# A retention layer and a PReLU feed-forward layer: the second product of blocks 1 to 5 computed as seven products of quarters

## The chip, the cores and the metric

The kernel runs on one core of a Trainium2 chip. The metric is the device time of one launch in microseconds (us), lower is better. Engines are named as the profile names them: PE (TensorE, matmuls), PEld (its weight loads), DVE (VectorE), ACT (ScalarE), POOL (GpSimd), SP (SyncE, which here only issues DMAs).

## The reference

Inputs are float32: q, k and v of 4 batches, 8 heads, 768 steps and 64 channels; two weight matrices of 512 x 2048 and 2048 x 512; and a vector alpha of 2048. The output is float32, 3072 x 512.

```python
# first layer, for each batch b and head h
state = gamma[h] * state + outer(k[t], v[t])
y[t] = scale * q[t] @ state
# second layer, over the 3072 tokens x (heads side by side)
h = x @ w_in
g = max(h, 0) + alpha * min(h, 0)
out = g @ w_out
```

## The kernel before

**Tiling.** The sequence of each batch is cut in three units of 256 steps, 12 units in all. Two units make a block of 512 tokens, so there are six blocks, n = 0 to 5. Matrix inputs are in 16 bits (float16), sums in PSUM in 32 bits. PSUM has eight banks of 128 x 512 32-bit values; the kernel names the bank of every tile by hand.

**First layer, per unit u.** `load(u)` reads k, q and v by DMA (SP). `rescale` multiplies k and q by powers of gamma into `kdq`, and `cast_v` makes `vx` in 16 bits (mostly POOL). `turn_pe` (early units) or `turn_dma` (a transposing DMA on SP's queue, from unit 4 on) makes the transposed `kq`. `sum_mm` makes the unit's two state sums (tiles `st0`, `st1`); `state` adds them on DVE to the running state (`ss`), multiplies by the decay on POOL (`tf`) and casts the result into `tg` (POOL or ACT). `score_mm` makes the scores of half the heads in two banks, and `masks` multiplies these on DVE by the causal mask. `out_mm` multiplies state and masked scores out, and `take_y` copies the result to `xT` on ACT.

**Second layer, per block n.** `ffn1(n)` makes 16 chunks of h (tile `hps`, four matmuls each). For each, ACT writes `hm` = relu(-h), and DVE writes a chunk of `gt` = hm x (1 - alpha) + h, which is g. Chunks of the first blocks are in part made one unit at a time, with 256 columns (`apart`). `ffn2(n)` multiplies: for each of four groups of 128 tokens (tq), 16 matmuls of 512 columns over the chunks of `gt`, a copy to `os` on ACT, and a store on SP's queue. In block 5 the last group is made in two halves of 256 columns.

**Order.** The kernel writes the order of every engine by hand (`manual_schedule`): each engine carries out its instructions in the order in which the program issues them. The tile library adds semaphore waits where data or buffers need them; a tile with `bufs=k` has k buffers in turn, and the tile after k others waits until all use of the first is over. `ffn1` and `ffn2` are generators that yield after each matmul; `tick(gen, m)` runs m of them, and so places the first layer's work for the next block between the matmuls of the second layer. The stretch at the end of block 0 matters here: there `ffn2(0)` (generator `gen`), the parts of `ffn1(1)` (generator `half`) and the first layer of units 2 and 3 alternate, and on SP's queue `turn_dma(4)` and `load(6)` stand ahead of the four stores of block 0.

**Tiles.** `os` has six buffers, the staged `ks`, `qs` and `vs` four each, `gt` two, `hm` three.

Of the kernel before, what the change touches and what calls it, by code (L numbers as in the profile page):

```python
# [20 lines left out]
def kernel(  # L21
# [68 lines left out]

    tgbuf = [sbp.tile([128, NP, 128], F16, tag=f"tg{i}", name=f"tg{i}") for i in range(6)]

    staged, prepped, live, tgs, xT, gts = {}, {}, {}, {}, {}, {}
    held = []

    def hold(ins):
        if held:
# [9 lines left out]
    def load(u, parts="kqv"):  # L107
        b, c = divmod(u, UPB)
        t = staged.setdefault(u, {})
        for nm in parts:  # L110
            src = {"k": k, "q": q, "v": v}[nm[0]]
            if nm[0] not in t:
                t[nm[0]] = sbp.tile(
                    [128, H, 2 * D], FP, tag=f"{nm[0]}s", bufs=4, name=f"{nm[0]}s{u}"
                )
            h = slice(0, H) if len(nm) == 1 else slice(4 * int(nm[1]), 4 * int(nm[1]) + 4)
            hold(
                nc.sync.dma_start(  # L118
                    out=t[nm[0]][:, h, :],
                    in_=src[b, h, U * c : U * c + U, :].rearrange(  # L120
                        "h (p r) d -> p h (r d)", r=2
                    ),
                )
            )
# [10 lines left out]
    def rescale(eng, u, t, h0, h1):  # L135
        kdq = unit(u)[0]
        at = OQ * t
        eng.tensor_tensor(  # L138
            out=kdq[:, t, :, h0:h1, :].rearrange("p r h d -> p h r d"),
            in0=staged[u]["kq"[t]][:, h0:h1, :].rearrange("p h (r d) -> p h r d", r=2),  # L140
            in1=tab[:, at + 2 * h0 : at + 2 * h1]
            .rearrange("p (h r) -> p h r", r=2)
            .unsqueeze(3)
            .to_broadcast([128, h1 - h0, 2, D]),
            op=MULT,
        )
# [160 lines left out]
    def take_y(u, cs):  # L307
# [4 lines left out]
        for c in cs:  # L312
# [7 lines left out]
                scale=1.0,  # L320
            )

    def ffn1(n, banks, apart=0):
# [5 lines left out]
        turns += [(f, 1, 0, 2) for f in range(apart, NFT)]  # L329
        for i, (f0, nf, lo, hi) in enumerate(turns):  # L330
            hps = ps(banks[i % len(banks)], "hps").rearrange("p (f t) -> p f t", f=nf)
            for f in range(nf):
                for hp in range(4):
                    nc.tensor.matmul(  # L334
                        out=hps[:, f, :].rearrange("p (u t) -> p u t", t=U),
                        lhsT=w_in_all[:, hp, 128 * (f0 + f) : 128 * (f0 + f) + 128],
                        rhs=xT[n][:, lo:hi, hp, :],
                        start=(hp == 0),
                        stop=(hp == 3),
                    )  # L340
# [4 lines left out]
            nc.scalar.activation(out=hm, in_=hps, func=RELU, bias=0.0, scale=-1.0)  # L345
            for f in range(nf):
                nc.vector.scalar_tensor_tensor(  # L347
                    out=gt[:, f0 + f, U * lo : U * hi],
                    in0=hm[:, f, :],
                    scalar=oma_sb[:, f0 + f : f0 + f + 1],  # L350
                    in1=hps[:, f, :],
                    op0=MULT,
                    op1=ADD,
                )
            yield

    def ffn2(n, banks, parts=1):
        gt = gts.pop(n)
        opss = {}
        step = NFT // parts  # L360
        for f0 in range(0, NFT, step):
            for tq in range(3 if n == NBLK - 1 else 4):
                if f0 == 0:
                    opss[tq] = ps(banks[tq % len(banks)], "ops")
                for ft in range(f0, f0 + step):
                    nc.tensor.matmul(  # L366
                        out=opss[tq],
                        lhsT=gt[:, ft, 128 * tq : 128 * tq + 128],
                        rhs=w_out_all[:, ft, :],
                        start=(ft == 0),  # L370
                        stop=(ft == NFT - 1),
                    )
                    if ft == NFT - 1:
                        os_sb = sbp.tile([128, d_model], FP, tag="os", bufs=6, name="os")
                        nc.scalar.activation(  # L375
                            out=os_sb, in_=opss[tq], func=COPY, bias=0.0, scale=1.0
                        )
                        row = TB * n + 128 * tq
                        nc.sync.dma_start(out=out[row : row + 128, :], in_=os_sb)
                    yield  # L380

        if n < NBLK - 1:
            return

        row = TB * n + 384
        for half in range(2):
            ops = ps(banks[1 + half], "ops")[:, 0:256]
            for ft in range(NFT):
                nc.tensor.matmul(  # L389
                    out=ops,  # L390
                    lhsT=gt[:, ft, 384:512],
                    rhs=w_out_all[:, ft, 256 * half : 256 * half + 256],
                    start=(ft == 0),
                    stop=(ft == NFT - 1),
                )
                yield
            for x in range(half + 1):
                w = 256 // (half + 1)
                os_sb = sbp.tile([128, d_model], FP, tag="os", bufs=6, name="os")[:, 0:w]
                i = ops[:, w * x : w * x + w]  # L400
                if x == 0:
                    nc.scalar.activation(out=os_sb, in_=i, func=COPY, bias=0.0, scale=1.0)
                else:
                    nc.vector.tensor_copy(out=os_sb, in_=i)
                at = 256 * half + w * x
                (nc.sync, nc.scalar)[x].dma_start(
                    out=out[row : row + 128, at : at + w], in_=os_sb
                )
# [137 lines left out]
    masks(3, 0)  # L546
    sum_mm(3, (6, 7))
    state(3, 0, G, "ga")
    tick(gen, 8)
    score_mm(3, 1, (4, 5))  # L550
    masks(3, 1)
    rescale(G, 4, 0, 0, 8)
    state(3, 1, G)
    rescale(G, 4, 1, 0, 8)
    cast_v(G, 4)
    turn_dma(4)
    load(6)
    rescale(G, 5, 0, 0, 8)
    rescale(G, 5, 1, 0, 8)
    cast_v(G, 5)  # L560
    tick(gen, 8)
    out_mm(3, (6, 7))
    tick(gen)
    turn_dma(5)
    load(7)
    tick(half)


    for n in range(1, NBLK):
# [36 lines left out]


# [28 lines left out]
```

## Time and profile before

| | |
|---|---|
| median of three runs | 212.03 us (211.62 to 212.3) |
| the profiled execution | 212.65 us, of it 210.9 us span from first to last instruction |
| TensorE's granted clock | 1.000 on average |
| busy | PE 202.7 us (96%), DVE 118.0 (56%), ACT 98.8 (47%), POOL 82.6 (39%) |
| second product (L366, L389) | 368 matmuls of 512 columns, 32 of 256 |
| first product (L334) | 336 matmuls of 512 columns, 96 of 256 |

The profile is one execution. Busy time of PE counts a matmul from its start to its modelled end, and matmuls overlap: the time from start to start, or the length of a run of them in the chain, says what each costs. Instruction groups give the source line, engine, operation, shapes, count, busy time and mean nanoseconds of one, and then the idle time of the engine ahead of them. In a timeline the first two numbers are start and length in us.

### The profile page before, as it was taken

The page shows a single profiled execution, that of the slowest core. Times are in us where ns is not written, and L with a number is a line of the kernel's source. Part 1 is how long each engine was busy: PE and PEld are TensorE (multiplying, and loading weights), DVE is VectorE, ACT ScalarE, POOL GpSimd, SP SyncE. Part 2 cuts the span into 40 slices and gives each one's busy share as a digit, 9 for nine tenths or more (in the row PEclk, how much of TensorE's full clock was granted, in tenths as well). Part 3 has the DMA queues.
Part 4 walks back from the last instruction along what each step waited for, and adds up shares of the span by engine and source line. Part 5 has one row for each costly group of instructions (what it writes and reads, how often), then busy time and mean ns, then how long its engine had stood idle before and what let it go on. Part 6 is the DMA issues. An engine that isn't in the chain of part 4 may idle for free.

```text
span 210.9 us, 4992 instructions
## 1 busy us (share of the span) xinstructions
PE 202.7 (96%) x2090; PEld 106.7 (51%) x2090; DVE 118.0 (56%) x194; ACT 98.8 (47%) x160; POOL 82.6 (39%) x104
## 2 busy tenths in 40 slices
PE   7799999997999999999999999999999999999993
PEld 2457545583564555444555444555444555444462
DVE  7785986354378831488740488740588640588000
ACT  2375665362667132666133566133665133665121
POOL 2389066464791599100499300499100610000000
PEclk9999999999999999999999999999999999999999
DMA  5999999999969991599521599521630111100112
GB/s 164 338 215 150 211 271 163 226 264 314 284 164 368 209 356 64 138 289 262 163 104 50 149 289 242 183 88 53 171 79 0 50 57 50 50 0 3 50 70 79
DMA packets 62407, 33.91 MB, mean 161 GB/s; under 512 B 18081, under 2 KB 59441, under 8 KB 62385
## 3 DMA queue, kind: packets, MB, share of 16 engines
q1 hardware_dynamic: 57840, 29.30, 48.8%
q0 software_dynamic: 4224, 4.19, 12.5%
q8 instruction: 16, 0.26, 0.5%
q10 hardware_dynamic: 320, 0.10, 0.2%
q14 instruction: 7, 0.05, 0.1%
HBM read 27.30 MB, written 6.29 MB: 159 GB/s over the span
## 4 chain that ended last, share of the span: by engine, by line
PE 77%; DMA 16%; POOL 1%; ACT 1%; DVE 1%; SPq 1%; issue 1%; POOLq 0%
PE ops L366 34%; PE hps L334 31%; DMA vs<-in_v_dram 5%; DMA wout<-in_moe_w_out_dram 4%; DMA ks<-in_k_dram 4%; DMA win<-in_moe_w_in_dram 3%; PE y L295 2%; PE kps L87 2%; PE ops L389 2%; PE y L280 2%; PE sca L251 2%; PE st L201 1%; ACT kq L174 1%; SPq L118 1%; PE scb L251 1%
## 5 line engine op out<-in xcount | busy, mean ns | idle before, releaser
L347 DVE SCALAR_TENSOR_TENSOR gt<-hm,oma,hps 128x512 f16<-128x512 f32 (+1 forms) x108 | 73.1, 688 | 50.9 <-ACT hm L345 41.9
L334 PE MATMUL hps<-xT,win 128*128 128x512 f16 (+1 forms) x432 | 84.3, 355 | 0.0
L366 PE MATMUL ops<-wout,gt 128*128 128x512 f16 x368 | 83.7, 379 | 0.0
L345 ACT ACTIVATE hm<-hps 128x512 f32<-128x512 f32 x96 | 57.3, 597 | 26.4 <-PE hps L334 26.3
L334 PEld LDWEIGHTS <-win 128*128 128x128 f16 x432 | 42.1, 98 | 40.8
L366 PEld LDWEIGHTS <-gt 128*128 128x128 f16 x368 | 34.5, 98 | 40.2
L375 ACT ACTIVATE os<-ops 128x512 f32<-128x512 f32 x23 | 13.6, 599 | 52.9 <-PE ops L366 52.9
L226 POOL TENSOR_TENSOR tf<-ss,tab 128x256 f32<-128x256 f32 x16 | 10.2, 636 | 44.6 <-DVE ss L225 44.0
L263 DVE TENSOR_TENSOR m<-sca,mi 128x512 f16<-128x512 f32 x24 | 16.5, 686 | 17.3 <-PE scb L251 17.3
L138 POOL TENSOR_TENSOR kdq<-ks,tab 128x1024 f16<-128x1024 f32 (+1 forms) x12 | 19.3, 1612 | 7.8 <-DMA ks<-in_k_dram 7.5
L239 POOL CAST tg<-tf 64x256 f16<-64x256 f32 x35 | 13.8, 394 | 21.2 <-DVE tf L222 19.5
L313 ACT ACTIVATE xT<-y 128x512 f16<-128x512 f32 x24 | 16.2, 740 | 11.1 <-PE y L295 11.1
L138 POOL TENSOR_TENSOR kdq<-qs,tab 128x1024 f16<-128x1024 f32 (+1 forms) x13 | 20.4, 1571 | 1.7 <-DMA qs<-in_q_dram 1.5
L154 POOL CAST vx<-vs 128x1024 f16<-128x1024 f32 (+1 forms) x13 | 12.6, 972 | 9.7 <-DMA vs<-in_v_dram 9.7
L263 DVE TENSOR_TENSOR m<-scb,mi 128x512 f16<-128x512 f32 x24 | 16.3, 681 | 0.0
L174 ACT ACTIVATE kq<-trb 128x1024 f16<-128x1024 f16 x8 | 8.2, 1022 | 5.9 <-PE trb L168 5.8
L87 PE MATMUL kps<-spin 128*128 128x512 f16 x25 | 8.5, 480 | 1.9 <-DVE spin L432 1.5
L225 DVE TENSOR_TENSOR ss<-tf,st 128x256 f32<-128x256 f32 x16 | 6.7, 416 | 5.7 <-PE st L201 4.8
L251 PE MATMUL sca<-kq 64*64 64x128 f16 x192 | 8.2, 218 | 1.2 <-ACT kq L174 1.1
L251 PE MATMUL scb<-kq 64*64 64x128 f16 x192 | 8.3, 219 | 0.0
L251 PEld LDWEIGHTS <-kq 64*64 64x64 f16 x384 | 6.1, 106 | 4.2 <-ACT kq L174 2.9
L295 PE MATMUL y<-m,vx 64*64 64x128 f16 x384 | 7.7, 219 | 0.0
(33 smaller groups left out, 67.7 us busy)
## 6 DMA issues: line engine op xcount, KB each, us to landing
out_dram<-os SPq DMA_DIRECT2D x23, 256.0 KB, 2.0
vs<-in_v_dram SPq DMA_DIRECT2D x10, 512.0 KB, 6.5
ks<-in_k_dram SPq DMA_DIRECT2D x8, 512.0 KB, 4.5
qs<-in_q_dram SPq DMA_DIRECT2D x8, 512.0 KB, 5.4
ks<-in_k_dram SPq DMA_DIRECT2D x8, 256.0 KB, 5.1
qs<-in_q_dram SPq DMA_DIRECT2D x8, 256.0 KB, 5.2
win<-in_moe_w_in_dram POOLq DMA_DIRECT2D x4, 512.0 KB, 5.8
wout<-in_moe_w_out_dram POOLq DMA_DIRECT2D x4, 512.0 KB, 9.1
```

Source lines behind the costliest of these rows:

```text
L87: nc.tensor.matmul(out=pt, lhsT=spin[:, 0:128], rhs=spin, start=True, stop=True)
L138: eng.tensor_tensor(out=kdq[:, t, :, h0:h1, :].rearrange("p r h d -> p h r d"), in0=staged[u]["kq"[t]][:, h0:h1, :].rearrange("p h (r d) - ...
L154: eng.tensor_copy(out=o, in_=i)
L239: nc.gpsimd.tensor_copy(out=o, in_=i)
L251: nc.tensor.matmul(out=scs[a][rows(c), at : at + 128], lhsT=kv[rows(a), 0, r, p, rows(c)], rhs=qmove(kq, a, c, p), start=True, stop=True,)
L263: nc.vector.tensor_tensor(out=m2, in0=live[u, hh][a].rearrange("p (r a i) -> p r a i", r=2, a=2), in1=mask.unsqueeze(2).to_broadcast([128, ...
L313: nc.scalar.activation(out=xT[n][:, ul, :, 128 * c : 128 * c + 128].rearrange("k a (p r) -> k a r p", r=2), in_=ys[c].rearrange("k (a r p) ...
L334: nc.tensor.matmul(out=hps[:, f, :].rearrange("p (u t) -> p u t", t=U), lhsT=w_in_all[:, hp, 128 * (f0 + f) : 128 * (f0 + f) + 128], rhs=x ...
L345: nc.scalar.activation(out=hm, in_=hps, func=RELU, bias=0.0, scale=-1.0)
L347: nc.vector.scalar_tensor_tensor(out=gt[:, f0 + f, U * lo : U * hi], in0=hm[:, f, :], scalar=oma_sb[:, f0 + f : f0 + f + 1], in1=hps[:, f, :],
L366: nc.tensor.matmul(out=opss[tq], lhsT=gt[:, ft, 128 * tq : 128 * tq + 128], rhs=w_out_all[:, ft, :], start=(ft == 0), stop=(ft == NFT - 1),)
L375: nc.scalar.activation(out=os_sb, in_=opss[tq], func=COPY, bias=0.0, scale=1.0)
```

## The change

From block 1 on `ffn2_seven` takes the place of `ffn2`. It cuts g in four quarters by units and by halves of d_ff, and w_out in four by halves of d_ff and d_model, and makes the block's output from seven products of quarters (Strassen's scheme in Winograd's form), each of 16 matmuls of 256 columns. Where the scheme adds products, TensorE adds into the same bank (0 or 1), ACT keeps a copy of what is there (`cu`), and DVE adds two of them (`plus`) into `os`. Four sums of quarters of w_out are made once on DVE (`w_sums`, tile `wsum`), four sums of quarters of g in each block (`g_sums`, which share the two buffers of `gt`).

With this, `ffn1` makes its chunks in the order 0, 8, 1, 9 and so on for n > 1 and has another list of banks; the tick counts, the banks of `out_mm` and `score_mm`, and the place of `state`, `masks` and `rescale` in the program change; a `rescale` in each block is made to wait for the last sum on DVE (`behind`); two `cast_v` move to ACT; `os` goes from six buffers to three, and the staged tiles from four to three. Block 5's output ends in `last`.

```diff
-                    [128, H, 2 * D], FP, tag=f"{nm[0]}s", bufs=4, name=f"{nm[0]}s{u}"
+                    [128, H, 2 * D], FP, tag=f"{nm[0]}s", bufs=3, name=f"{nm[0]}s{u}"
...
+    def w_sums(i, lo, hi):
+        w = w_out_all.rearrange("p (k f) (j e) -> p k f j e", k=2, j=2)
+        w12, w21, w22 = w[:, 0, lo:hi, 1, :], w[:, 1, lo:hi, 0, :], w[:, 1, lo:hi, 1, :]
+        t1, t2, t3, t4 = (wsum[:, x, lo:hi, :] for x in range(4))
+        o, a, b = (
+            (t1, w12, w[:, 0, lo:hi, 0, :]), (t2, w22, t1), (t3, w22, w12), (t4, w21, t2)
+        )[i]
+        return nc.vector.tensor_tensor(out=o, in0=a, in1=b, op=SUB)
...
+    def g_sums(n, i, lo, hi):
+        if n not in gsums:
+            gsums[n] = sbp.tile([128, 4, HF, U], F16, tag="gt", bufs=2, name=f"gs{n}")
...
+        o, a, b, op = (
+            (s1, a21, a22, ADD), (s2, s1, a11, SUB), (s3, a11, a21, SUB), (s4, a12, s2, SUB)
+        )[i]
+        return nc.vector.tensor_tensor(out=o, in0=a, in1=b, op=op)
...
+        rest = range(apart, NFT)
+        if apart == 0:
+            rest = [f + x for f in range(HF) for x in (0, HF)]
...
+            if n > 0 and f0 in (HF + 5, NFT - 1):
+                lo, hi = (0, 6) if f0 < NFT - 1 else (6, HF)
+                g_sums(n, 0, lo, hi)
+                g_sums(n, 1, lo, hi)
             yield
...
-                        os_sb = sbp.tile([128, d_model], FP, tag="os", bufs=6, name="os")
+                        os_sb = sbp.tile([128, d_model], FP, tag="os", bufs=3, name="os")
...
+    def ffn2_seven(n, x, y, z=None):
...
+        ox = bank(x, "ox")
+        yield from product(ox, gq(0, 0), wq(0, 0), True)
+        c1 = kept(ox)
+        yield
+        oy = bank(y, "oy")
+        yield from product(oy, gq(1, 0), wq(1, 0), True)
+        store(0, 0, plus(oy, c1))
+        yield
+        yield from product(ox, gs(1), ws(1), False)
+        u2 = kept(ox)
+        yield
+        oy = bank(y, "oy")
+        yield from product(oy, gs(0), ws(0), True)
+        if z is not None:
+            u5 = plus(oy, u2, "cu")
+        yield
+        yield from product(ox, gs(2), ws(2), False)
+        u3 = kept(ox)
+        store(1, 1, plus(oy, u3))
+        yield
+        if z is not None:
+            oz = bank(z, "oz")
+            yield from product(oz, gs(3), wq(1, 1), True)
+            store(0, 1, plus(oz, u5))
+            yield
+            yield from product(ox, gq(1, 1), ws(3), False, lambda m: last(n, ox, m))
+            yield
+        else:
+            yield from product(ox, gq(1, 1), ws(3), False)
...
+            store(1, 0, c21)
+            yield
+            yield from product(oy, gs(3), wq(1, 1), False)
+            store(0, 1, plus(oy, u2))
+            yield
...
     state(3, 0, G, "ga")
+    w_sums(0, 0, HF)
+    for i in range(1, 4):
+        w_sums(i, 0, 4)
     tick(gen, 8)
     score_mm(3, 1, (4, 5))
     masks(3, 1)
-    rescale(G, 4, 0, 0, 8)
     state(3, 1, G)
+    for i in range(1, 4):
+        gate = w_sums(i, 4, HF)
+    behind(rescale(G, 4, 0, 0, 8), gate)
     rescale(G, 4, 1, 0, 8)
-    cast_v(G, 4)
+    cast_v(A, 4)
     turn_dma(4)
     load(6)
...
-    cast_v(G, 5)
     tick(gen, 8)
     out_mm(3, (6, 7))
     tick(gen)
     turn_dma(5)
     load(7)
+    tick(half, 8)
+    cast_v(A, 5)
     tick(half)
...
-            gen = ffn1(n, (4, 5, 6, 7, 0, 1))
+            gen = ffn1(n, (7, 2, 3, 1, 0, 6, 5, 4, 7, 1, 0, 4, 5, 6, 7, 1))
             if more:
                 for u in (u0, u0 + 1):
-                    tick(gen, 8)
-                    rescale(G, u, 0, 0, 8)
+                    i = rescale(G, u, 0, 0, 8)
+                    if u == u0:
+                        behind(i, gate)
...
+                    tick(gen, 8)
             tick(gen)
-        gen = ffn2(n, (0, 1) if more else (0, 1, 2))
+        gen = ffn2_seven(n, 0, 1, None if more else 2)
         if more:
-            tick(gen, 7)
+            tick(gen, 8)
             sum_mm(u0, (2, 3))
             sum_mm(u0 + 1, (2, 3), half=1)
             score_mm(u0, 0, (4, 5))
             score_mm(u0, 1, (6, 7))
             state(u0, 0, G)
             masks(u0, 0)
+            masks(u0, 1)
+            tick(gen, 25)
             state(u0, 1, G)
-            masks(u0, 1)
             state(u0 + 1, 0, G)
             state(u0 + 1, 1, G)
-            tick(gen, 25)
-            out_mm(u0, (2, 3))
-            score_mm(u0 + 1, 0, (4, 5))
-            score_mm(u0 + 1, 1, (6, 7))
+            g_sums(n, 2, 0, HF)
+            tick(gen, 16)
+            out_mm(u0, (4, 5))
+            score_mm(u0 + 1, 0, (6, 7))
+            score_mm(u0 + 1, 1, (2, 3))
             masks(u0 + 1, 0)
             masks(u0 + 1, 1)
-            tick(gen, 22)
-            out_mm(u0 + 1, (2, 3))
+            gate = g_sums(n, 3, 0, HF)
+            tick(gen, 32)
+            out_mm(u0 + 1, (4, 5))
+        else:
+            g_sums(n, 2, 0, HF)
+            g_sums(n, 3, 0, HF)
         tick(gen)
```

More of the change, by code (lines that the diff above doesn't have):

```diff
@@ L12 @@
 COPY = mybir.ActivationFunctionType.Copy
+SUB = mybir.AluOpType.subtract
 RELU = mybir.ActivationFunctionType.Relu
@@ L79 @@
     w_out_all = sbp.tile([128, NFT, d_model], F16, tag="wout", name="wout")
+    HF, HM = NFT // 2, d_model // 2
+    wsum = sbp.tile([128, 4, HF, HM], F16, tag="wsum", name="wsum")
     def ps(bank, name, dt=FP, n=512):
@@ L91, with behind @@
     tgbuf = [sbp.tile([128, NP, 128], F16, tag=f"tg{i}", name=f"tg{i}") for i in range(6)]
-    staged, prepped, live, tgs, xT, gts = {}, {}, {}, {}, {}, {}
+    staged, prepped, live, tgs, xT, gts, gsums = {}, {}, {}, {}, {}, {}, {}
     held = []
+    def behind(ins, other):
+        tc.add_manual_dep(
+            ins.ins,
+            other.ins.name,
+            mybir.DependencyInfo(
+                mybir.DependencyClass.Sync, mybir.DependencyReason.DATA
+            ),
+            reason="one engine of two at the second read port",
+        )
     def hold(ins):
@@ L137, in rescale @@
         at = OQ * t
-        eng.tensor_tensor(
+        return eng.tensor_tensor(
             out=kdq[:, t, :, h0:h1, :].rearrange("p r h d -> p h r d"),
@@ L321, in take_y @@
             )
+    def w_sums(i, lo, hi):
[9 more added lines that the diff above has]
+            gsums[n] = sbp.tile([128, 4, HF, U], F16, tag="gt", bufs=2, name=f"gs{n}")
+        g = gts[n].rearrange("p (k f) (j t) -> p k f j t", k=2, j=2)
+        a11, a12 = g[:, 0, lo:hi, 0, :], g[:, 1, lo:hi, 0, :]
+        a21, a22 = g[:, 0, lo:hi, 1, :], g[:, 1, lo:hi, 1, :]
+        s1, s2, s3, s4 = (gsums[n][:, x, lo:hi, :] for x in range(4))
+        o, a, b, op = (
+            (s1, a21, a22, ADD), (s2, s1, a11, SUB), (s3, a11, a21, SUB), (s4, a12, s2, SUB)
+        )[i]
+        return nc.vector.tensor_tensor(out=o, in0=a, in1=b, op=op)
     def ffn1(n, banks, apart=0):
@@ L328, in ffn1 @@
         turns = [(f, 2, ul, ul + 1) for ul in range(2) for f in range(0, apart, 2)]
-        turns += [(f, 1, 0, 2) for f in range(apart, NFT)]
+        rest = range(apart, NFT)
+        if apart == 0:
+            rest = [f + x for f in range(HF) for x in (0, HF)]
+        turns += [(f, 1, 0, 2) for f in rest]
         for i, (f0, nf, lo, hi) in enumerate(turns):
@@ L361, in ffn2 @@
         for f0 in range(0, NFT, step):
-            for tq in range(3 if n == NBLK - 1 else 4):
+            for tq in range(4):
                 if f0 == 0:
@@ L380, in ffn2, with gq, gs, wq @@
                     yield
[L382 to L408, printed above, removed]
+    def ffn2_seven(n, x, y, z=None):
+        g = gts[n].rearrange("p (k f) t -> p k f t", k=2)
+        w = w_out_all.rearrange("p (k f) d -> p k f d", k=2)
+        def gq(k, ul):
+            return lambda f, m: g[:, k, f, U * ul + 128 * m : U * ul + 128 * m + 128]
+        def gs(i):
+            return lambda f, m: gsums[n][:, i, f, 128 * m : 128 * m + 128]
+        def wq(k, j):
+            return lambda f: w[:, k, f, HM * j : HM * j + HM]
+        def ws(i):
+            return lambda f: wsum[:, i, f, :]
+        def bank(i, name):
+            return ps(i, name).rearrange("p (m e) -> p m e", m=2)
+        def product(o, lhs, rhs, first, after=None):
+            for m in range(2):
+                for f in range(HF):
+                    nc.tensor.matmul(
+                        out=o[:, m, :],
+                        lhsT=lhs(f, m),
+                        rhs=rhs(f),
+                        start=(first and m == 0 and f == 0),
+                        stop=(f == HF - 1),
+                        skip_group_check=True,
+                    )
+                    if f == HF - 1 and after is not None:
+                        after(m)
+                    if m == 0 or f < HF - 1:
+                        yield
+        def kept(o):
+            t = sbp.tile([128, 2, HM], FP, tag="cu", bufs=3, name="cu")
+            nc.scalar.activation(out=t, in_=o, func=COPY, bias=0.0, scale=1.0)
+            return t
+        def plus(o, t, name="os"):
+            so = sbp.tile([128, 2, HM], FP, tag=name, bufs=3, name=name)
+            nc.vector.tensor_tensor(out=so, in0=o, in1=t, op=ADD)
+            return so
+        def store(i, j, t):
+            nc.sync.dma_start(
+                out=out[TB * n + U * i : TB * n + U * i + U, HM * j : HM * j + HM].rearrange(
+                    "(m p) d -> p m d", m=2
+                ),
+                in_=t,
+            )
+        ox = bank(x, "ox")
[27 more added lines that the diff above has]
+            yield from product(ox, gq(1, 1), ws(3), False)
+            c21 = sbp.tile([128, 2, HM], FP, tag="os", bufs=3, name="os")
+            nc.scalar.activation(out=c21, in_=ox, func=COPY, bias=0.0, scale=1.0)
+            store(1, 0, c21)
+            yield
+            yield from product(oy, gs(3), wq(1, 1), False)
+            store(0, 1, plus(oy, u2))
+            yield
@@ new lines, in last @@
+    def last(n, o, m):
+        row = TB * n + U + 128 * m
+        for x in range(m + 1):
+            e = HM // (m + 1)
+            t = sbp.tile([128, 2, HM], FP, tag="os", bufs=3, name="os")[:, 0, 0:e]
+            i = o[:, m, e * x : e * x + e]
+            if x == 0:
+                nc.scalar.activation(out=t, in_=i, func=COPY, bias=0.0, scale=1.0)
+            else:
+                nc.vector.tensor_copy(out=t, in_=i)
+            (nc.sync, nc.scalar)[x].dma_start(
+                out=out[row : row + 128, e * x : e * x + e], in_=t
+            )
@@ L592 @@
             masks(u0, 0)
+            masks(u0, 1)
+            tick(gen, 25)
             state(u0, 1, G)
-            masks(u0, 1)
             state(u0 + 1, 0, G)
             state(u0 + 1, 1, G)
-            tick(gen, 25)
-            out_mm(u0, (2, 3))
-            score_mm(u0 + 1, 0, (4, 5))
-            score_mm(u0 + 1, 1, (6, 7))
+            g_sums(n, 2, 0, HF)
[3 more added lines that the diff above has]
+            score_mm(u0 + 1, 1, (2, 3))
             masks(u0 + 1, 0)
             masks(u0 + 1, 1)
-            tick(gen, 22)
-            out_mm(u0 + 1, (2, 3))
+            gate = g_sums(n, 3, 0, HF)
+            tick(gen, 32)
+            out_mm(u0 + 1, (4, 5))
+        else:
+            g_sums(n, 2, 0, HF)
+            g_sums(n, 3, 0, HF)
         tick(gen)
```

## The prediction

> **What bounds the kernel now.** I read the page's busy shares first, then the chain of waits in order of time, then the groups by shape, and last the timelines of the stretch in which block 0 ends.
>
> ```profile
> span 210.9 us, 4992 instructions
> ...
> PE 202.7 (96%) x2090; PEld 106.7 (51%) x2090; DVE 118.0 (56%) x194; ACT 98.8 (47%) x160; POOL 82.6 (39%) x104
> ```
> TensorE is busy 96% of the span. The chain, start and length in us, shows what a matmul costs when they follow one another:
>
> ```profile
> 1.52 4.45 PE kps L87 x10
> ...
> 85.65 13.81 PE hps L334 x64
> ...
> 102.06 5.50 PE ops L366 x25
> ...
> 203.90 3.51 PE ops L389 x32
> ```
> 512 columns take 0.216 us (13.81/64), 256 columns 0.110 us (3.51/32, with a new weight tile for each, as the change has it). From 85 us on the chain is TensorE alone, one block in 31.3 us (85.65 to 116.94). The first ten spin matmuls took 0.445 us each: TensorE starts from rest at half its later rate.
>
> ```profile
> L263 DVE TENSOR_TENSOR m<-sca,mi 128x512 f16<-128x512 f32 x24 | 16.5, 686 | 17.3 <-PE scb L251 17.3
> ...
> L448 DVE MEMSET tg<- 128x256 uint32 x6 | 1.6, 272 | 0.0
> ...
> L432 DVE MEMSET spin<- 128x512 f16 x1 | 0.5, 485 | 1.0 <-PEq L620 1.0
> ```
> These price the sums (mean ns after the bar). The last three views (start, length) are ScalarE, GpSimd and SP's queue while block 0's second product ends:
>
> ```profile
> 53.98 0.60 ACT L375 ACTIVATE os<-ops 128x512 f32<-128x512 f32 x1 [2.06 <-PE ops L366]
> 54.84 0.60 ACT L375 ACTIVATE os<-ops 128x512 f32<-128x512 f32 x1 [0.27 <-PE ops L366]
> 55.98 1.34 ACT L313 ACTIVATE xT<-y 128x512 f16<-128x512 f32 x2 [0.55 <-PE y L295]
> 57.17 1.09 ACT L375 ACTIVATE os<-ops 128x512 f32<-128x512 f32 x2
> 58.54 0.60 ACT L345 ACTIVATE hm<-hps 128x512 f32<-128x512 f32 x1 [0.28 <-PE hps L334]
> ```
> ```profile
> 51.90 1.89 POOL L138 TENSOR_TENSOR kdq<-ks,tab 128x1024 f16<-128x1024 f32 x1
> ...
> 56.58 1.90 POOL L138 TENSOR_TENSOR kdq<-qs,tab 128x1024 f16<-128x1024 f32 x1
> ```
> ```profile
> 58.51 1.71 SPq L158 DMA_TRANSPOSE kq<-kdq  x1
> 60.27 0.57 SPq L118 DMA_DIRECT2D ks<-in_k_dram  x1
> ...
> 62.71 3.58 SPq L379 DMA_DIRECT2D out_dram<-os  x4
> ```
> ```profile
> out_dram<-os SPq DMA_DIRECT2D x1, 256.0 KB, 5.7
> ```
> The first `os` is copied out of PSUM by 54.6 us, but its store is issued at 62.71: SP stands at turn_dma(4), which needs GpSimd's rescale of unit 4 (done 58.48), and then at load(6). The last line is that store from issue to landing (window 62.7 to 63 us): landed at 68.4. Today nobody waits for it: `os` has six buffers.
>
> **The change, part by part.** Sums are made against the profiled execution's own 212.65 us (span 210.9 and 1.75 around it), which is 0.3% above the median of the three runs, 212.03.
>
> *Products.* Per block 64 x 0.216 = 13.8 becomes 7 x 16 = 112 x 0.110 = 12.3: minus 1.52 us for n=1 to 4; in n=5 48 in 10.36 and 3.51 become 12.3: minus 1.58. All on the path: **-7.7**.
>
> *Price of a sum.* No 16-bit two-tensor sum from SBUF is in the trace. Above, masks (0.15 + 1.047 ns an element): 2.28 us for 2048 elements. Below, VectorE wrote 512 16-bit values as 256 words in 272 ns against 485: at that 0.83 ns a word, 0.91 us. I take a mask's cost for a pair as one element: 0.15 + 1024 x 1.047 = 1.22 us; 0.95 for 1536, 0.68 for 1024, 0.42 for 512. The memset row says that pairs can go as words, so I stay near that end.
> The Trainium skill, "VectorE: DVE Perf Modes", section on the perf-mode tier table, gives 2x for a 16-bit tensor_tensor in SBUF, 1224 ns for 2048, and 1x for any operand in PSUM, which is what the mask row is. By it the sum stands as below; by the plain mask row it is the first rival.
>
> *`os` from six buffers to three: the largest term.* The fourth `os` of block 0 (the second at 57.17) now needs the first one's store landed. That would be 68.4 even with all else as now, and the change moves it later: rescale(4) is put behind w_sums. VectorE: t1 from 51.42 to 52.6, three halves to 54.6, masks(3,1) to 55.8 (out_mm(3) waits 0.3), ss to 56.1, three halves to 58.0. GpSimd's two rescales then end at 61.8 and SP repeats its order 3.3 us later: store 66.0, landed 71.7. ScalarE has one order, so behind this copy stand all hm of block 1's other first-product turns, and behind those VectorE's gt. (cast_v(4) on ScalarE waits for its load, 46.40 + 7.6 = 54.0, and moves the first copies 1.1 us, under matmuls that do not need them.) TensorE goes on from 57.7 with turns 4 to 8 of `half`, 4 x 0.88 + 0.86, and at 62.1 needs bank 3, which holds the uncopied result. Copy done 72.35; turn 9 starts; turn 10 needs bank 0, so hm and gt of turns 4 to 6, queued with cast_v(5): 76.2. Then six turns of 0.863: end 81.4, against 67.8 now. TensorE has rested 10 us; by the spin row a restart cost 4.45 - 2.16 = 2.3 us; turn 9's share lies under the wait, and I take two turns at half rate, 1.7. **+15.3** (bounds 10, with the 2.0 us of most stores and no restart, and 16).
> The Trainium skill, "TensorE: Matmul & The Clock Gate", Part 1, has the array at half clock after an idle window, for some 3.4 us. By that page 1.7 us are lost here, an estimate; the granted clock in this profile never falls, so no run shows it yet.
>
> *s1 and s2 inside the first product.* In time from the end of ffn1's matmuls (99.30 in the block shown), the last gt ends at 1.59 and turn 11's at -1.86. s1, s2 over six chunks (2 x 0.95) go in there, so turn 14's gt ends at 2.24 (back to back 0.67 apart), where it now ends at 0.73. With the new order of chunks (0, 8, 1, 9 ...) turn 14 is chunk 7, read by the eighth matmul of the first product, due at 0.77. Wait **1.5** in n=2 to 5; in n=1 (chunks in order) score_mm(u0,1) waits 1.6 for bank 7 instead: **+7.6**. Bounds by the price: 5.1 and 15.6.
>
> *Same bank twice running.* Product 5 and product 6 both add into bank 0, and u3 must be copied between: 0.16 until the last matmul lands, 0.04, 0.60 copy (ScalarE's os row), 0.05. tick counts 8+25+16+32 = 81 put product 6's first matmul ahead of out_mm, so nothing fills this: 0.85 x 4 (n=5 has another product between): **+3.4**.
>
> *Bank 2 and 3.* score_mm(u0+1,1) now needs the banks that hold the states until VectorE's last ss. ss waits for GpSimd's tf and tg (1.5 us a step). With one step (n=1, 4) or none (n=3) it is ready at 8.8, TensorE at 9.25; n=2 has two steps, 10.3: **+1.1**. In n=5 s3 and s4 stand before the first `plus`: **+0.25**.
>
> *Hidden.* The other plus (0.69), s3, s4, and masks end 1 to 2 us ahead of their readers in n=1 to 4; VectorE has 18.3 of 31.3 us busy now, and adds 4 x 1.2 to 1.4 and 2.1. Uncovered, each costs its own length. The tail after the last matmul (128-wide copies, two stores) stays. In the later blocks the gate moves rescale (9.7 us of GpSimd) 4 us later, SP's transposes behind it; they land some 8 us before score_mm, as the second transpose is now issued in the middle of ffn1.
>
> Sum: -7.7 + 15.3 + 7.6 + 3.4 + 1.1 + 0.25 = +20.0; 212.65 + 20.0 = 232.65, and 0.3% lower on the median's scale: **232**.
>
> **Rivals.**
> 1. *Sums at an element each* (the mask row): the gate comes 4.3 later, s1 and s2 hold each block 3.1, s3 about 0.4, n=5 2.9 instead of 0.25: about 249. Against it the memset row. Chance 0.09.
> 2. *Only the held copy bites*: VectorE's sums fit ahead of their readers and the bank waits close: 212.65 - 7.7 + 15.3 = 220.3, so 219.7. For it, VectorE idles 7.4 us before each ffn1; against it, the order of chunks above. 0.08.
> 3. *The fourth copy is not held* (the store lands before 62.1): 217. Against it, 62.71 for the issue even now. 0.07.
> 4. *TensorE sets the end and everything added hides in the other engines' idle time*: 205, faster. The place is block 0's end and each first product; it decides if the store lands by 62.1 and s2 ends before turn 12's gt is due, at -1.0. For it, the 96%; against it, both times above. 0.04.
>
> **How the numbers follow.** The forecast has 0.72. Its range, from the bounds of the copy and of the sums, is 223 to 237. To hold 0.8 the whole range takes in rival 2 and, above, a sum price between the two rows: 219 to 240. A measurement here can tell about 0.3%: faster by more only in rival 4, 0.04; within it 0.01; slower 0.95.
>
> **What would show it.** In the profile after: the fourth ScalarE copy of block 0 starts after an idle of over 10 us, right when the first store lands, and TensorE's idle in that stretch is as long; 256-column matmuls 0.110 us apart; sums of 2048 at 1.2 us; the eighth matmul of a first product waits about 1.5 us for gt, and product 6's first about 0.85 for ScalarE. If that copy starts by 62 us, or the sums take 2.3 us, the prediction is wrong at its largest or its second term.

## The result and the profile after

| | before | after |
|---|---|---|
| median, measured side by side (us) | 212.17 (211.62 to 214.88) | 233.57 (232.65 to 236.69) |
| ratio to before | | 1.0947 (95% interval 1.0881 to 1.1013) |
| the profiled execution, and its span | 212.65, 210.9 | 232.69, 231.0 |
| TensorE's granted clock, mean | 1.000 | 0.968 |

The medians are of all executions; the ratios, here and below, leave out on both sides those over 1.5% above the fastest of their kernel.

The change makes the kernel about 9.5% slower. The forecast was 232 us (219 to 240), so it holds; whether its reasons hold is the question of the rest.

The busy line of the page first, and from its table of slices the row of the granted clock:

```profile
span 231.0 us, 5497 instructions
...
PE 199.8 (86%) x2314; PEld 128.8 (56%) x2314; DVE 157.1 (68%) x247; ACT 100.2 (43%) x162; POOL 86.5 (37%) x102
...
PEclk9999999999965699999999999999999999999998
```

TensorE has a little less work, as the scheme promises, but is busy 86% of the span instead of 96%, and in three slices in the middle its clock is down, where before the row reads 9 throughout. The chain of waits (start and length in us) has both halves of the story:

```profile
66.53 5.56 DMA out_dram<-os
72.19 0.60 ACT os L419
...
76.45 5.11 PE hps L374 x16
...
114.53 0.96 DVE gs L358
...
129.53 0.61 ACT cu L468
...
133.21 1.75 PE oy L453 x16
```

Above, a store and a copy stand in the chain ahead of `hps`. Below, in block 2, VectorE's sums (`gs`) and a copy to `cu` stand between products, where before the chain was TensorE alone. A product is 1.75 us for 16 matmuls, 0.109 us each, where the prediction took 0.110.

The sums by shape (count: minimum/median/maximum in ns, start of first and last, shapes):

```profile
L358 DVE TENSOR_TENSOR gs<-gt,gs x5: 1212/1215/1216, 95.5 to 217.4; 128x2048 f16<-128x2048 f16 x5
...
L345 DVE TENSOR_TENSOR wsum<-wout x3: 679/1095/1215, 51.1 to 56.3; 128x1024 f16<-128x1024 f16 x2, 128x2048 f16<-128x2048 f16 x1
```

2048 elements cost 1.21 us and 1024 cost 0.68 us when nothing disturbs them. The 1.09 us in the second line is a disturbed one of 1024, beside GpSimd's casts; more of that at the end.

Now the timelines that were shown of before, ScalarE, GpSimd and SP's queue, then that store from issue to landing (window 66 to 67 us), and TensorE's timeline besides, where block 0's second product ends.

```profile
58.13 0.60 ACT L419 ACTIVATE os<-ops 128x512 f32<-128x512 f32 x1
72.19 0.60 ACT L419 ACTIVATE os<-ops 128x512 f32<-128x512 f32 x1 [13.46 <-DMA out_dram<-os]
```
```profile
58.58 1.90 POOL L152 TENSOR_TENSOR kdq<-ks,tab 128x1024 f16<-128x1024 f32 x1
60.44 1.90 POOL L152 TENSOR_TENSOR kdq<-qs,tab 128x1024 f16<-128x1024 f32 x1
```
```profile
62.37 1.71 SPq L172 DMA_TRANSPOSE kq<-kdq  x1
...
66.53 6.62 SPq L423 DMA_DIRECT2D out_dram<-os  x4
```
```profile
out_dram<-os SPq DMA_DIRECT2D x1, 256.0 KB, 5.6
```
```profile
55.96 0.38 PE L294 MATMUL y<-kq,tg 128*128 128x128 f16 x4 [1.42 <-DVE ss L239]
...
58.36 4.52 PE L374 MATMUL hps<-xT,win 128*128 128x256 f16 x36
72.84 1.86 PE L374 MATMUL hps<-xT,win 128*128 128x512 f16 x4 [9.95 <-ACT os L419]
76.45 6.82 PE L374 MATMUL hps<-xT,win 128*128 128x512 f16 x24 [1.75 <-DVE gt L387]
83.10 1.04 PE L453 MATMUL ox<-wout,gt 128*128 128x256 f16 x8
```

The fourth copy of block 0 starts 13.46 us after the end of the third, at the moment when the first store of `os` has landed (66.53 + 5.56 = 72.09). TensorE waits 9.95 us for it, then 1.75 us for what ScalarE and VectorE had queued, and its first matmuls after that run slowly. The first product of block 1 starts at 83.10 us. Before, TensorE had no such hole, and it started at 67.80:

```profile
57.40 10.56 PE L334 MATMUL hps<-xT,win 128*128 128x256 f16 x64
67.80 1.67 PE L366 MATMUL ops<-wout,gt 128*128 128x512 f16 x7
```

These **15.3 us** are three quarters of the 20.1 us between the spans. The remaining 4.8 us lie in the five blocks that follow, 147.9 us from there to the end against 143.1.

There TensorE waits at a few places: in blocks 2 to 5 at the eighth matmul of the first product, in block 1 twice in `score_mm` instead (0.66 and 0.45 us for `gt`), in block 2 alone at a later matmul of `score_mm`, and in blocks 1 to 4 at the first matmul of product 6 (TensorE's timeline, block 2):

```profile
117.52 0.28 PE L453 MATMUL ox<-wout,gt 128*128 128x256 f16 x1 [1.03 <-DVE gt L387]
...
125.59 0.21 PE L265 MATMUL scb<-kq 64*64 64x128 f16 x1 [1.06 <-DVE ss L239]
...
130.18 0.27 PE L453 MATMUL ox<-wsum,gt 128*128 128x256 f16 x1 [0.69 <-ACT cu L468]
```

### The profile page after: what moved, and what is told of

It reads as the page before. It is cut to its first block, busy times and chain, and to the rows that moved or that the text cites. A ratio compares the mean times of both kernels' runs of the same rounds, so it can differ in the third digit from the quotient of the medians.

```text
span 231.0 us, 5497 instructions
## 1 busy us (share of the span) xinstructions
PE 199.8 (86%) x2314; PEld 128.8 (56%) x2314; DVE 157.1 (68%) x247; ACT 100.2 (43%) x162; POOL 86.5 (37%) x102
## 3 DMA queue, kind: packets, MB, share of 16 engines
q0 software_dynamic: 4224, 4.19, 11.4%
## 4 chain that ended last, share of the span: by engine, by line
PE 63%; DVE 17%; DMA 6%; ACT 4%; POOL 4%; SPq 3%; issue 2%; DVEq 0%; POOLq 0%; ACTq 0%
PE hps L374 28%; PE ox L453 13%; PE oy L453 10%; DVE gt L387 6%; DVE gs L358 4%; PE ops L410 3%; DMA out_dram<-os 3%; SPq L132 2%; DMA ks<-in_k_dram 2%; PE y L309 2%; DVE wsum L345 2%; ACT hm L385 2%; DVE m L277 2%; PE y L294 2%; POOL kdq L152 2%
## 5 line engine op out<-in xcount | busy, mean ns | idle before, releaser
L453 PEld LDWEIGHTS <-gs 128*128 128x128 f16 x320 | 31.0, 98 | 3.9
L453 PEld LDWEIGHTS <-gt 128*128 128x128 f16 x240 | 22.7, 98 | 10.9 <-DVE gt L387 6.0
L468 ACT ACTIVATE cu<-ox 128x512 f32<-128x512 f32 x15 | 9.0, 597 | 44.0 <-PE ox L453 44.0
L253 POOL CAST tg<-tf 64x256 f16<-64x256 f32 x35 | 19.3, 550 | 17.9 <-DVE tf L236 16.2
L152 POOL TENSOR_TENSOR kdq<-ks,tab 128x1024 f16<-128x1024 f32 (+1 forms) x12 | 19.4, 1614 | 15.6 <-DMA ks<-in_k_dram 9.6
L473 DVE TENSOR_TENSOR os<-oy,cu 128x512 f32<-128x512 f32 x14 | 9.7, 690 | 19.4 <-PE oy L453 16.3
L453 PE MATMUL ox<-wsum,gs 128*128 128x256 f16 x160 | 19.1, 273 | 0.0
L453 PE MATMUL ox<-wout,gt 128*128 128x256 f16 x80 | 11.6, 274 | 4.2 <-DVE gt L387 4.1
L410 PE MATMUL ops<-wout,gt 128*128 128x512 f16 x64 | 15.2, 380 | 0.0
L358 DVE TENSOR_TENSOR gs<-gt 128x1536 f16<-128x1536 f16 (+2 forms) x15 | 13.0, 868 | 0.3
L453 PE MATMUL ox<-wsum,gt 128*128 128x256 f16 x80 | 10.4, 273 | 3.2 <-ACT cu L468 2.7
```

The costliest lines, as they stand in the source:

```text
L152: return eng.tensor_tensor(out=kdq[:, t, :, h0:h1, :].rearrange("p r h d -> p h r d"), in0=staged[u]["kq"[t]][:, h0:h1, :].rearrange("p h ...
L253: nc.gpsimd.tensor_copy(out=o, in_=i)
L358: return nc.vector.tensor_tensor(out=o, in0=a, in1=b, op=op)
L410: nc.tensor.matmul(out=opss[tq], lhsT=gt[:, ft, 128 * tq : 128 * tq + 128], rhs=w_out_all[:, ft, :], start=(ft == 0), stop=(ft == NFT - 1),)
L453: nc.tensor.matmul(out=o[:, m, :], lhsT=lhs(f, m), rhs=rhs(f), start=(first and m == 0 and f == 0), stop=(f == HF - 1), skip_group_check=True,
```

## The experiments

The stretch up to about 50 us waits for loads, and its length differs by some us between executions. So beside the ratio of whole times each experiment is read by two inner lengths of its profiled execution: **(a)** from VectorE's `tf` that opens the stretch with the held copy (50.73 in after, 51.05 before) to the first product of block 1, and **(b)** from that product to the end of the span. Before, they are 16.75 and 143.1 us; after, 32.37 and 147.9.

| kernel | edit | median us | ratio to before (95%) | (a) us | (b) us |
|---|---|---|---|---|---|
| 1 | fourth copy has a buffer of `cu` | 219.06 | 1.0267 (1.0176 to 1.0357) | 18.04 | 147.9 |
| 2 | before, with three `os` | 226.81 | 1.0537 (1.0392 to 1.0682) | 28.18 | 143.1 |
| 3 | spins in the hole | 235.40 | 1.1019 (1.0908 to 1.1130) | 33.43 | 147.8 |
| 4 | rescale not gated, put earlier | 234.78 | 1.1002 (1.0893 to 1.1111) | 33.81 | 147.8 |
| 5 | 1, and product 6 behind `out_mm` | 215.63 | 1.0110 (1.0038 to 1.0182) | 18.03 | 145.2 |
| 6 | 1, and the sums behind the last `gt` | 219.83 | 1.0296 (1.0234 to 1.0357) | 18.03 | 148.0 |
| 7 | all of it reordered | 213.25 | 0.9963 (0.9921 to 1.0004) | 16.83 | 141.8 |
| 8 | 7, and a load behind a transpose | 212.08 | 0.9867 (0.9804 to 0.9929) | 17.14 | 139.7 |
| 9 | 8, and two states on VectorE | 211.52 | 0.9884 (0.9840 to 0.9929) | 16.83 | 139.8 |

Kernels 1 to 4, 5 to 7, and 8 and 9 each shared their runs of before. The profiled execution of kernel 2 began late, and so did that of 9; the (b) of kernel 2, where nothing was changed, is that of before all the same.

**1. The held copy alone.** `cu` has three buffers that are idle in block 0.

```diff
-  os_sb = sbp.tile([128, d_model], FP, tag="os", bufs=3, name="os")
+  os_sb = sbp.tile([128, d_model], FP, tag="os" if tq < 3 else "cu", bufs=3, name="os")
```

> The changed kernel, but block 0's fourth copy takes a buffer of cu, idle then, instead of the os buffer whose store is still out. Theory (the held copy is the largest term, 15.3 us with the restart of TensorE): the fourth copy runs near 58 us, the granted clock stays at full, and the profiled time falls by 15 us to about 217.4. Rival (the seven products and the sums themselves are the loss, the copy's wait is mostly hidden): no more than 3 us come back, about 230.

ScalarE's and TensorE's timelines of kernel 1:

```profile
59.69 1.09 ACT L421 ACTIVATE os<-ops 128x512 f32<-128x512 f32 x2
```
```profile
59.92 10.56 PE L374 MATMUL hps<-xT,win 128*128 128x256 f16 x64
70.33 1.04 PE L455 MATMUL ox<-wout,gt 128*128 128x256 f16 x8
```

The third and fourth copies follow at once, TensorE runs all 64 matmuls in one go at full clock, and (a) is 14.33 us shorter than in after; (b) does not move. So the buffer of the fourth copy holds 14.3 of the 15.6 us by which (a) had grown, and the rival that put it at 3 us or less falls. What is left in (a) is 18.04 - 16.75 = 1.29 us, and all of it has come by the start of out_mm(3): 5.23 us after that `tf` here (57.52), 3.94 before (54.99).

**2. The same hold in the kernel before.** Both `os` lines with `bufs=3`, nothing else.

> The kernel before with os at three buffers and nothing else changed. Theory: the first store lands at 68.4 as now, so the fourth copy starts there and not at 57.7; TensorE stops at its tenth first-product turn from 62 to 69 us, restarts at half rate, and the time grows by about 10.7 us, to 223 (9 without the slow restart). Rival (the buffers cost little alone; the gate behind the sums of w_out makes the wait): within 2 us of 212.

ScalarE's and TensorE's timelines of kernel 2:

```profile
72.41 0.60 ACT L375 ACTIVATE os<-ops 128x512 f32<-128x512 f32 x1 [10.84 <-DMA out_dram<-os]
```
```profile
73.06 1.86 PE L334 MATMUL hps<-xT,win 128*128 128x512 f16 x4 [7.33 <-ACT os L375]
76.02 8.10 PE L334 MATMUL hps<-xT,win 128*128 128x512 f16 x24 [1.10 <-DVE gt L347]
```

The hole opens without any of the seven products, and the first product starts at 83.96: (a) is 11.4 us longer than before, where 10.7 was expected; the ratio of the whole times, 5.4%, comes to about as much. One word of the change, three for six, is its largest single cost; what after has on top of it (32.37 - 28.18 = 4.19 in (a)) is the smaller part.

**3. The price of the restart.** 44 spin matmuls keep TensorE busy while it waits.

```diff
+    tick(half, 28)
+    keep(44, 7)
     tick(half)
```

> The changed kernel with 44 spin matmuls (9.5 us) after the ninth turn of block 1's first product, where TensorE waits for the held copy. Theory (1.7 us of that term are the restart at half rate): the granted clock stays at full there, turn 9 takes 0.86 us, and the time falls by 1.6 to 2 us, to about 231. Rival (the rest costs nothing, turns are bound by gt): no change within 0.3 us.

Windows of 4 us; after the busy times (PE, PEld, DVE, ACT, POOL) come the granted clock, the DMA share and GB/s. First after, then kernel 3:

```profile
72.00:76.00 4.00, 1.86 (x4) 0.40 (x3) 2.13 (x6) 3.77 (x7) 0.00 (x0) 0.50 0.84 240
76.00:80.00 4.00, 3.55 (x10) 1.36 (x11) 3.24 (x7) 1.67 (x4) 0.00 (x0) 0.57 0.99 274
```
```profile
72.00:76.00 4.00, 2.38 (x12) 0.97 (x10) 0.00 (x0) 1.02 (x3) 0.00 (x0) 1.00 0.70 252
76.00:80.00 4.00, 1.41 (x6) 0.38 (x4) 3.35 (x9) 3.66 (x7) 0.00 (x0) 0.82 0.89 214
80.00:84.00 4.00, 4.00 (x15) 1.64 (x14) 2.78 (x4) 1.79 (x3) 0.00 (x0) 0.75 1.10 330
```

No gain, and the test failed to do what it was for. The spins held the clock at 1.00 until 76 us, but the store took 6.8 us to land instead of 5.6, so the spins ran out 1.62 us too early, TensorE then rested 2.59 us for `gt`, and the clock fell afterwards. The last 24 matmuls of the first product took 6.53 us against 6.65: the restart was moved, not taken away, and what a kernel without it would gain is not shown by this run.

**4. The gate.** The first `rescale` of unit 4 ahead of `state(3, 1)` and without `behind`.

```diff
+    rescale(G, 4, 0, 0, 8)
     state(3, 1, G)
...
-    behind(rescale(G, 4, 0, 0, 8), gate)
```

> The changed kernel with the rescale of unit 4 back ahead of state(3,1) and without its wait for the last sum of w_out. Theory (the gate moved the first store by 3.3 us): the store lands near 68.4 and the time falls by 3.3, to about 229.4. Rival (GpSimd's rescale and VectorE's sums of two SBUF operands hold each other up, so the masks and the rescale come later): the fall is under 2 us, and the sums or the rescale beside each other are longer than 0.68 and 1.90 us.

VectorE's, GpSimd's and SP's timelines of kernel 4:

```profile
51.35 0.42 DVE L236 TENSOR_TENSOR tf<-st,tab 128x256 f32<-128x256 f32 x1
...
52.94 2.63 DVE L345 TENSOR_TENSOR wsum<-wout,wsum 128x1024 f16<-128x1024 f16 x1
```
```profile
53.13 1.89 POOL L152 TENSOR_TENSOR kdq<-ks,tab 128x1024 f16<-128x1024 f32 x1
58.45 0.93 POOL L240 TENSOR_TENSOR tf<-ss,tab 128x256 f32<-128x256 f32 x1 [3.42 <-DVE ss L239]
...
61.07 1.90 POOL L152 TENSOR_TENSOR kdq<-qs,tab 128x1024 f16<-128x1024 f32 x1
```
```profile
67.24 6.70 SPq L423 DMA_DIRECT2D out_dram<-os  x4
```

The store is issued 15.89 us after that `tf`, against 15.80 in after: the rival held. GpSimd's second `rescale` stands behind `tf` and `tg`, these wait for `ss`, and `ss` stands behind the sums on VectorE, gate or no gate. The run also shows what the earlier `rescale` costs VectorE: a sum of 1024 beside it takes 2.63 us, where the same sum took 0.77 in after, and what stands behind it, `ss` too, is 1.9 us later. That (a) is 1.44 us longer than in after is another thing: 1.27 of it lie in the last 24 matmuls of the first product, which ran longer at the lower clock (7.92 us against 6.65).

**5. Product 6 behind `out_mm`.** Kernel 1, with one tick less:

```diff
-            tick(gen, 32)
+            tick(gen, 31)
             out_mm(u0 + 1, (4, 5))
```

> The kernel with the fourth copy freed, and one tick fewer (31, not 32) ahead of the second out_mm, so that out_mm and not product 6 follows product 5. Theory (product 6 waits 0.85 us in each of four blocks for the copy of the bank that product 5 left): out_mm covers it, and from the first product of block 1 to the end the time falls by 3.4 us, from 147.9 to 144.5. Rival (out_mm waits as long for the masks or for the state): under 1 us.

TensorE's timeline of kernel 5:

```profile
112.93 1.91 PE L455 MATMUL ox<-wsum,gs 128*128 128x256 f16 x16
114.68 0.61 PE L294 MATMUL y<-kq,tg 128*128 128x128 f16 x8
...
115.79 1.92 PE L455 MATMUL ox<-wsum,gt 128*128 128x256 f16 x16
```

The wait for `cu` is gone: `out_mm` runs while ScalarE copies. (b) falls by 2.7 of the 3.4 us; 0.46 us came back as a wait for a `kq` transfer in block 1. This is one number in the program, and it is worth over half of the 4.8 us that the blocks had lost.

**6. The sums behind the last `gt`.** Kernel 1, chunks in plain order, s1 and s2 whole and behind the last chunk.

```diff
-        if apart == 0:
-            rest = [f + x for f in range(HF) for x in (0, HF)]
...
-            if n > 0 and f0 in (HF + 5, NFT - 1):
-                lo, hi = (0, 6) if f0 < NFT - 1 else (6, HF)
-                g_sums(n, 0, lo, hi)
-                g_sums(n, 1, lo, hi)
+            if n > 0 and f0 == NFT - 1:
+                g_sums(n, 0, 0, HF)
+                g_sums(n, 1, 0, HF)
```

> The kernel with the fourth copy freed, chunks in plain order in every block, and s1 and s2 whole behind the last gt, nothing else changed. Theory: the first product no longer waits (1.4 us a block gone), but the masks and the plus behind the sums come later, and product 4 waits about 1.2 us for plus; net 0 to 0.5 us a block, 146 to 148 from the first product of block 1 to the end. In block 5, where s3 and s4 stand there too, no gain. Rival (the sums were only in the wrong place): the full 1.4 us a block, about 141.

VectorE's and TensorE's timelines of kernel 6:

```profile
103.79 1.22 DVE L358 TENSOR_TENSOR gs<-gt 128x2048 f16<-128x2048 f16 x1
105.05 1.23 DVE L358 TENSOR_TENSOR gs<-gs,gt 128x2048 f16<-128x2048 f16 x1
```
```profile
109.65 0.27 PE L452 MATMUL oy<-wsum,gs 128*128 128x256 f16 x1 [0.87 <-DVE os L472]
...
112.78 0.21 PE L265 MATMUL scb<-kq 64*64 64x128 f16 x1 [1.38 <-DVE ss L239]
```

The first product no longer waits, as expected, but (b) stays at 148.0: `plus` (on VectorE at 108.91) now stands behind both sums and four masks, so bank 1 comes free late, and product 4 waits 0.87 us; the states are later too. A sum taken out of one wait turned up in the next, because VectorE carries out its work in one order and TensorE asks for it in each product.

**7, 8 and 9. Everything reordered.** Kernel 7 takes kernel 6's sums, lets `masks(u0, 1)` and the states follow behind `plus`, puts two products ahead of `out_mm(u0)` and product 6 behind `out_mm(u0 + 1)`, moves the first halves of `w_sums` 2 and 3 behind `state(3, 1)`, and gives block 5's half copies a buffer of `hm` in place of `os`. Its core:

```diff
             masks(u0, 0)
+            tick(gen, 24)
             masks(u0, 1)
-            tick(gen, 25)
...
             g_sums(n, 2, 0, HF)
-            tick(gen, 16)
+            tick(gen, 32)
             out_mm(u0, (4, 5))
...
             gate = g_sums(n, 3, 0, HF)
-            tick(gen, 32)
+            tick(gen, 16)
             out_mm(u0 + 1, (4, 5))
         else:
+            tick(gen, 32)
```

> All of it together: the fourth copy freed; plain order of chunks; s1 and s2 behind the last gt; plus of product 2 ahead of the second pair of masks; products 3 and 4 ahead of out_mm(u0), product 5 ahead of out_mm(u0+1); s3 and s4 of block 5 behind its first plus; the first half of the sums of w_out behind state(3,1); the last copies into buffers of hm. Theory (what is lost is lost to waits that an order can hide): TensorE waits only about 2.2 us in block 2 and 1.2 in block 5, first product of block 1 to the end 138.6, about 208 in all, 2% faster than the kernel before. Rival (VectorE, with its sums, is the bound of a block): no faster than 212.

(a) is back at 16.83, as `ss` no longer waits for two of the sums. (b) is 141.8 us, below before's 143.1 for the first time, but 3.2 above what was expected, and the whole time is within 0.4% of before, not 2% below it. One reason is on TensorE's timeline of kernel 7:

```profile
78.84 0.24 PE L265 MATMUL sca<-kq 64*64 64x128 f16 x1 [1.67 <-DMA kq<-kdq]
```

Unit 5's transpose reaches its reader late in block 1; on SP's queue `load(6)` stands ahead of it. Kernel 8 moves that load behind `turn_dma(5)`:

```diff
     turn_dma(4)
-    load(6)
...
     turn_dma(5)
+    load(6)
     load(7)
```

> The reordered kernel, with load(6) moved on SP's queue from ahead of block 0's stores to behind turn_dma(5). Theory (in block 1 score_mm(5,0) waits 1.7 us for the transposed kq of unit 5, whose DMA stands behind that load and the stores): the transpose lands before it is read, and from the first product of block 1 to the end 141.8 becomes 140.1. Rival (the wait goes to load(7) or the rescale of unit 6 instead): under 0.3 us.

That wait is gone and (b) is 139.7, as expected: 3.4 us below before, and the ratio, 0.9867 (0.9804 to 0.9929), lies below 1 with its whole interval. What is left in block 2 are waits for the states and, behind them, for s3, as GpSimd hands each `tf` back to VectorE. Kernel 9 makes two of the `tf` on VectorE:

```diff
-            state(u0, 1, G)
-            state(u0 + 1, 0, G)
+            state(u0, 1, V)
+            state(u0 + 1, 0, V)
```

> The same, and the decay of two of the four states of a block on VectorE instead of GpSimd. Theory (block 2 waits 2 us for a chain of three ss with a tf on GpSimd, 1.5 us a step, between them): a step becomes 0.9 us, block 2 gains 0.8 to 1.2 us and the others nothing, 139 from the first product of block 1 to the end, 208 to 209 in all and faster than the kernel before. Rival (VectorE has no room there; each tf of 0.4 us pushes s3 and the masks): no gain, or a loss of up to 0.5 us a block.

The groups of TensorE's matmuls, kernel 8 and then kernel 9 (busy us, mean ns | idle before, by releaser):

```profile
L452 PE MATMUL ox<-wsum,gs 128*128 128x256 f16 x160 | 19.2, 273 | 2.0 <-DVE gs L358 1.6 <-ACT xT L327 0.4
...
L265 PE MATMUL scb<-kq 64*64 64x128 f16 x192 | 8.5, 219 | 1.2 <-DVE ss L239 1.2
```
```profile
L452 PE MATMUL ox<-wsum,gs 128*128 128x256 f16 x160 | 19.1, 273 | 2.9 <-DVE gs L358 2.9
...
L265 PE MATMUL scb<-kq 64*64 64x128 f16 x192 | 8.5, 219 | 0.4 <-DVE ss L239 0.4
```

The wait for `ss` falls by 0.8 us, the wait for `gs` grows by 1.3, and (b) is 139.8: the rival held, no gain that these runs can tell. The version that beats both kernels is 8 (or 9), by the ratio 1.2 to 1.3% faster than before; the medians, 212.08 and 211.52 against 212.40 for before in the same runs, differ by 0.2 and 0.4%.

## Why the prediction was right, and where it was not

The blocks first, from the start of a block's first product to the next `hps` (in block 5 to the last matmul), in us:

| block | before | after | difference | predicted |
|---|---|---|---|---|
| 1 | 17.69 | 18.46 | +0.77 | -1.52 + 1.6 + 0.85 = +0.93 |
| 2 | 17.48 | 19.42 | +1.94 | -1.52 + 1.5 + 0.85 + 1.1 = +1.93 |
| 3 | 17.47 | 18.11 | +0.64 | -1.52 + 1.5 + 0.85 = +0.83 |
| 4 | 17.68 | 18.33 | +0.65 | +0.83 |
| 5 | 14.02 | 14.40 | +0.38 | -1.58 + 1.5 + 0.25 = +0.17 |
| after the last matmul | 3.51 | 3.92 | +0.41 | 0 |

- **Products**: the price is right, 0.109 to 0.110 us a matmul. The 7.7 us cannot be read off alone, as the waits of the same blocks come to more.
- **Price of a sum**: right, and near the lower of its two bounds for 2048 elements (0.91 and 2.28 us). 1.21, 0.96, 0.68 and 0.42 us were measured for 2048, 1536, 1024 and 512 elements; 1.22, 0.95, 0.68 and 0.42 were taken. The rule of the Trainium skill ("VectorE: DVE Perf Modes", the perf-mode tier table), whose 1224 ns for 2048 stood beside the sum, agrees; the first rival, an element each, falls. So do the others: the copy was held, and blocks 1 to 5 lost 4.4 us, where the rivals without waits there have them win.
- **`os` from six buffers to three**: the mechanism and its size are right, and kernels 1 and 2 show them apart. Of its parts: the store was issued at 66.53 (66.0 predicted) and landed at 72.09 (71.7); turn 10 started at 76.45 (76.2); the 24 matmuls from there took 6.65 instead of 24 x 0.216 = 5.18, so 1.5 us were lost to the clock (1.7). Being 0.25 late at turn 10 and 0.2 cheap in the clock, they cancel.
- **What delays the store** failed in kind. The prediction gave 3.3 us to the place of `rescale` behind the w_sums. The fourth copy ends 22.06 us behind `tf` in after (72.79) and 17.23 in kernel 2 (73.01, its `tf` at 55.78), a difference of 4.83; and kernel 4 shows that without the gate it would not shrink, since the sums hold `ss` and a sum beside `rescale` is stretched. The prediction priced every sum as undisturbed.
- **out_mm(3)** waited 1.42 us, not 0.3: not for masks(3,1), but for the banks 6 and 7, from which `ss` had still to read the state sums behind the w_sums. It cost nothing in after, as TensorE stood for the store later anyway; in kernel 1, where it does not, it is the 1.29 us that are left in (a).
- **s1 and s2**: the eighth matmul shows 1.03 us of wait in block 2, and is 1.38 us behind its due time with the slower start of the seven ahead of it (117.52 against 116.14, by 0.110 us each from 115.37); 1.5 was predicted. In block 1 the two waits in `score_mm` come to 1.11 us, where 1.6 was predicted.
- **Same bank twice running**: right. Product 6 starts 0.85 us behind the time at which product 5's pace would have it start (130.18 against 127.58 + 16 x 0.109 = 129.33); of this 0.69 is shown as a wait, and kernel 5 takes it away.
- **Bank 2 and 3**: right, 1.06 us in block 2 (1.1), in no other.
- **Block 5**: its term was in the wrong place. Product 4 does not wait for s4; instead the second half of the last product waits 0.47 us for ScalarE's copy, and VectorE's last copy 2.33 us for a store, as `os` has three buffers there too. The tail, which "stays" by the prediction, grew by 0.4.
- **The total**, +20.0 against a measured 20.04 between the profiled executions, is closer than its parts, which is luck: (a) grew by 15.62, not 15.3, but after had reached its `tf` 0.32 us earlier, and the blocks came out 0.3 cheaper than their terms and the tail 0.4 dearer.

The clock: by "TensorE: Matmul & The Clock Gate" (Part 1) of the Trainium skill, the array is at half clock after a rest and until it has been busy for some 3.4 us. The trace now agrees in kind: granted 0.72 in 64 to 68 us, 0.50 in 68 to 76 and 0.57 in 76 to 80, from a rest of ten us. The loss is not one number: 1.5 us in after and 2.8 in kernel 2 (24 matmuls in 7.94 us), after rests of 9.95 and 7.33 us. Shorter windows show what sets it. The clock was down from 65.79 to 79.45 us in after, from 67.96 to 81.61 in kernel 2, from 69.14 to 82.80 in kernel 4 and from 78.57 to 81.98 in kernel 3: 13.66, 13.65, 13.66 and 3.41 us, that is four steps of 3.41 us in three kernels and a single one in kernel 3. The 24 matmuls had started 3.0, 5.6, 5.6 and 2.7 us before it came back (at 76.45, 76.02, 77.24 and 79.24), and they lost half of that each time: 1.5, 2.8, 2.7 and 1.35 us against 5.18. Where they had started 0.4 and 0.7 us into a step (after, kernel 3), the clock came back at the end of this step; where 1.2 and 1.3 us into it (kernels 2 and 4), only at the end of the next. In kernels 2 and 4 that made 5.6 us of matmuls without a pause at half clock, more than the 3.4 us of the Trainium skill; here the measurement decides. So in these runs the loss hangs on where in a step the restart falls, not on the length of the rest, and that 1.7 came near in after is luck; what sets the steps in time is not shown.

## What to carry to other kernels

Count buffers when a change takes some away: a copy that waits for a store waits for everything that stands ahead of this store on its queue, and in an in-order engine everything behind the copy waits too (here 14 us from three buffers). A saving of multiplications is paid in orders, not in additions: each undisturbed sum was as cheap as predicted, and what the blocks lost, they lost to what stood behind the sums on VectorE and to a bank used twice running. One buffer, and ticks, sums and a load moved by hand, turned 9.5% slower into about 1% faster with the same arithmetic. When one wait is taken away, follow the engine's order to the next reader before counting the gain, as kernels 6 and 9 show.

## What was not expected of the hardware

VectorE's sums with both operands in SBUF and GpSimd hold each other up. GpSimd's cast to `tg` takes 0.39 us alone (51.54 in before) and 1.33 beside a sum (started at 51.21 in after, in the sum of 51.07 to 52.29); its mean over the 35 casts rises from 394 to 550 ns, before and after:

```profile
L239 POOL CAST tg<-tf 64x256 f16<-64x256 f32 x35 | 13.8, 394 | 21.2 <-DVE tf L222 19.5
```
```profile
L253 POOL CAST tg<-tf 64x256 f16<-64x256 f32 x35 | 19.3, 550 | 17.9 <-DVE tf L236 16.2
```

The other way round the sum of 1024 in kernel 4 took 2.63 us beside a `rescale` of 1.89. Masks and `plus`, which have an operand in PSUM, keep their 0.67 to 0.69 us. The Trainium skill says so ("SBUF — State Buffer", section on who interferes with whom: VectorE with two SBUF inputs contends with a GpSimd instruction that reads SBUF, and who comes first holds the shared port), and these rows agree that they contend; in kernel 4 the sum, started at 52.94, came to its end only behind the cast and the `rescale` (53.13 to 55.02) beside it. The prediction left this out.

A store of 256 KB issued behind three loads took 5.6 us to land in after and 6.8 in kernel 3, where 2.3 is the median of all stores; the prediction had this from before (5.7). Kernels 7 and 8, which differ in the place of `load(6)` alone, show that the loads do it: behind them the first store is issued 15.68 us after `tf` and takes 7.3 us, ahead of them it is issued after 13.45 and takes 2.6 (kernel 8, window 64.4 to 65 us):

```profile
out_dram<-os SPq DMA_DIRECT2D x1, 256.0 KB, 2.6
```

So the tail of a queue costs twice, in being issued late and in landing among the loads. Whether moving `load(6)` would have shortened the hold in after, no run shows.
